# A small first load, a reordered root and one store fewer in the head of a fused scan and gated-MLP kernel

## The chip, the cores and the metric

The kernel runs on one core of one Trainium2 chip. The metric is the device time of one execution in microseconds; the median of three runs stands for a kernel. A core has TensorE (PE, matrix products), VectorE (DVE), ScalarE (ACT), GpSimd (POOL) and SyncE (SP). SyncE and ScalarE issue the kernel's plain loads, each from its own queue; the same 16 DMA engines move the data of both.

## The reference: what is computed

```python
xn = layernorm(x)                       # x: 2048 tokens x 448
s = 2.0 * real(hseq @ Cmat.T) + xn * Dskip   # hseq: h = Lam_bar * h + xn @ B_bar.T, token by token
h = sigmoid(xn @ w_gate) * (xn @ w_up)  # 448 -> 1792
g = silu(h @ w_down)                    # 1792 -> 448
out = x + s * g
```

Inputs and output are bfloat16. The change touches only how the first tokens are normalised and how the first columns of `w_gate` come in.

## The kernel before, in words

The 2048 tokens are 16 tiles of 128, in four chunks of 512. For each chunk TensorE does 14 gate and up steps (seven output pairs m for each of the two weights), the input product of the scan, the down product and the output product of the scan; VectorE does the scan itself and most evictions from PSUM.

**Order of work.** The kernel does not issue instructions directly. Each is added to a plan (`Plan.add`) with its engine, an estimated cost and the data that it reads and writes; `solve` then orders each engine's list by simulated times, and `emit` issues it. TensorE runs in program order. While `pl.seq` is set, which it is for the whole head, VectorE and ScalarE run in program order too. Loads go with `chain=True`, so each issuing queue keeps program order. `land` is the planner's figure for when a load arrives; it only steers the order.

**The head, chunk 0.** SyncE loads x tiles 0 and 2 (lines 402 and 404), ScalarE's queue tiles 1 and 3 (403 and 405). ScalarE's function table is loaded at 408. The first gate block is the first 256 of each half's 896 output columns. Its 448 input rows are seven groups of 64, and `load_w0` (line 374) brings them in four pieces: half 0 part A (three groups) and half 1 part A (four groups, on ScalarE's queue), then part B of half 0 (four groups) and of half 1 (three groups). Lines 409 to 412. Part A of both halves is what the matmuls marked "b" need; those marked "a" need part B too. After that SyncE issues the other gate blocks, more x tiles, and the up weights.

TensorE runs ten matmuls on constants at first (line 445). Tile 0's statistics are VectorE's (`stats`, 451 and 457) with the root on ScalarE (`root`, 485); tile 1's are ScalarE's (`act_mean` 489, `act_var` 493, `act_root` 497); tiles 2 and 3 are VectorE's with roots on ScalarE. A reciprocal (482) and a normalising step (531) on VectorE follow. Tile 0 is transposed by TensorE (569 and 571) into two banks, and ScalarE copies them out (579): first slots 4 to 6, after which the "b" matmuls run, then slots 0 to 3, after which the "a" matmuls run. Tiles 1 to 3 are transposed at 589 and 590, copied by ScalarE at 593, and shifted between partition halves by VectorE at 600. `last_tile` (826 and 827) does the gate matmuls of one tile: tile 0 "b", transposes of tile 1, tile 0 "a", transposes of tiles 2 and 3, then tiles 1, 2 and 3. From then on whole chunks are multiplied (808 and 809).

The small parameter rows, transposed by TensorE at 635 and 637 and copied at 642, are part of the head too. An output tile is finished in `yout` (1065 to 1067) and stored by SyncE (1056).

Of the kernel before, what the change touches and what calls it, by code (L numbers as in the profile page):

```python
# [14 lines left out]
ACT = mybir.ActivationFunctionType  # L15
# [3 lines left out]
D = 448  # L19
F = 1792  # L20
P = 128
H = 64
# [28 lines left out]
def dve2(n):  # L51
    return 0.067 + n / 1920.0


def dve1(n):
    return 0.067 + n / 960.0
# [17 lines left out]
class Plan:  # L74
# [10 lines left out]
    def add(self, eng, cost, fn, r=(), w=(), dma=0, lat=None, chain=False, name="", rate=230e3):  # L85
        o = Op()
        o.idx, o.eng, o.cost, o.fn, o.dma, o.name = len(self.ops), eng, cost, fn, dma, name
        o.lat = LAT.get(eng, 0.0) if lat is None else lat
        o.pre, o.suc, o.rate = {}, [], rate
        o.slot, o.land = None, 0.0  # L90
        if dma and eng != "POOL":
            o.slot, self.n_dma = self.n_dma, self.n_dma + 1
        o.start = o.end = None
        for k in r:
            if k in self.w:
                self._edge(self.w[k], o, True)
        for k in w:
            for q in self.r.get(k, ()):
                self._edge(q, o, False)
            if k in self.w:  # L100
                self._edge(self.w[k], o, True)
        for k in w:
            self.w[k] = o
            self.r[k] = []
        for k in r:
            if k not in w:
                self.r.setdefault(k, []).append(o)
        if chain or eng == "PE" or (eng in ("DVE", "ACT") and self.seq):
            key = ("chain", eng)
            if key in self.last_of:  # L110
                self._edge(self.last_of[key], o, None)
            self.last_of[key] = o
        self.ops.append(o)
        return o
# [132 lines left out]
def kernel(  # L247
# [18 lines left out]
    V, A, G, T, Q = nc.vector, nc.scalar, nc.gpsimd, nc.tensor, nc.sync  # L266
# [5 lines left out]
    def sbt(name, shape, dt=BF16):  # L272
        return sb.tile([P] + list(shape), dt, name=name)
# [10 lines left out]
    wgt = {"g": sbt("wG", [7, 896]), "u": sbt("wU", [7, 896])}  # L284
# [66 lines left out]
    add = pl.add  # L351
# [3 lines left out]
    def load(eng, key, nbytes, o, i, cost=0.45, r=(), rate=230e3, land=0.0):  # L355
        e = {"SP": Q, "ACT": A, "POOL": G}[eng]
        add(eng, cost, lambda: e.dma_start(out=o, in_=i), w=[key] if not isinstance(key, list) else key,  # L357
            r=r, dma=nbytes, chain=True, rate=rate).land = land

    def load_x(t0, n, q="SP", r=(), rate=230e3, land=0.0):  # L360
        load(q, [("x", t) for t in range(t0, t0 + n)], n * P * D * 2,
             x_all[:, t0:t0 + n, :], x_src[:, t0:t0 + n, :], r=r, rate=rate, land=land)
# [3 lines left out]
    def load_w(eng, k, half, b, r=(), rate=105e3, land=0.0):  # L366
        m0, m1 = BLK[k][b]
        ps = slice(half * H, half * H + H)
        c0 = half * 896
        load(eng, [("w", k, half, m) for m in range(m0, m1)], H * 7 * (m1 - m0) * P * 2,  # L370
             wgt[k][ps, :, m0 * P:m1 * P],
             wsrc[k][:, c0 + m0 * P:c0 + m1 * P].rearrange("(s p) f -> p s f", p=H), cost=0.65, r=r, rate=rate, land=land)

    def load_w0(eng, half, part, r=(), land=0.0):
        ps = slice(half * H, half * H + H)
        s0, c0 = (1 - half if part == "A" else half), half * 896
        n = 4 - s0
        load(eng, [("w", "g", half, m, part) for m in range(2)], H * n * 2 * P * 2, wgt["g"][ps, s0:7:2, 0:2 * P],
             wsrc["g"][:, c0:c0 + 2 * P].rearrange("(s p) f -> p s f", p=H)[:, s0:7:2, :], cost=0.5, r=r, rate=400e3, land=land)
# [21 lines left out]
    def load_p(eng, k, r=()):  # L401
        load(eng, ("vrow", k), D * 2, vrow[k:k + 1, :], (A_log_dt, A_Lambda_im, A_Lambda_re)[k].unsqueeze(0), cost=0.75 if eng == "POOL" else 0.45, r=r)
    load_x(0, 1, "SP")
    load_x(1, 1, "ACT")
    load_x(2, 1, "SP", rate=180e3)
    load_x(3, 1, "ACT", rate=180e3)
    load_p("SP", 2)
    add("ACT", 0.05, lambda: A.preload_act_table_set("sqrt_and_others"), w=["sqrttab"], lat=1.3, chain=True)
    load_w0("SP", 0, "A", land=5.7)
    load_w0("ACT", 1, "A", land=5.9)  # L410
    load_w0("SP", 0, "B", land=6.9)
    load_w0("SP", 1, "B", r=[("x", 1)], land=6.9)
    load_p("POOL", 0)
    load_p("POOL", 1)
    add("POOL", 0.15, lambda: G.memset(ident[:], 0.0), w=["ident"], chain=True)
    add("POOL", 0.4, lambda: G.affine_select(out=ident[:], in_=ident[:], compare_op=ALU.not_equal, fill=1.0, base=0,
                                             pattern=[[-1, P]], channel_multiplier=1), r=["ident"], w=["ident"], chain=True)
    add("POOL", 0.1, lambda: G.memset(wgt["g"][0:1, 0, 256:258], 0.0), w=[("w", "g", 0, m) for m in (2, 3)], chain=True)
    load_w("SP", "g", 0, 1, rate=400e3, land=8.8)
    load_w("SP", "g", 1, 1, rate=400e3, land=9.8)  # L420
    load_w("SP", "g", 0, 2, rate=400e3, land=11.2)
    load_w("SP", "g", 1, 2, rate=400e3, land=12.6)
    load_x(4, 2, land=14.0)
    add("POOL", 0.1, lambda: G.memset(halfc[:], 0.5), w=["consts"])
    add("POOL", 0.1, lambda: G.memset(negc[:], -1.0), r=["consts"], w=["consts"])
    add("POOL", 0.1, lambda: G.memset(expc[:], math.e), w=["expc"])
# [5 lines left out]
        w=[("xnw", t) for t in (1, 2, 3)])  # L432
# [16 lines left out]
    def bn(t):  # L449
        b = t % 3  # L450
        add("DVE", 0.56 if t < TPC else 0.6, lambda: V.bn_stats(out=bst[b][:], in_=x_all[:, t, :]),
            r=[("x", t)] + ([("xnT", 0, 3, "a")] if 3 < t < 8 else []), w=[("bst", b)])

    def aggr(t):
        b = t % 3
        o = (mvf if t < TPC else mv)[:, t, :]
        add("DVE", 0.1 if t < TPC else 0.16, lambda: V.bn_aggr(out=o, in_=bst[b][:]), r=[("bst", b)], w=[("mv", t)])

    def stats(t):
        bn(t)  # L460
        aggr(t)
# [22 lines left out]
    def root(t):  # L484
        add("ACT", 0.2, lambda: A.activation(sdb[:, t, :], mvf[:, t, 1:2], ACT.Sqrt, bias=epsc[:]),
            r=[("mv", t), "sqrttab", "epsc"], w=[("sd", t)], lat=0.16)

    def act_mean(t):
        add("ACT", 0.62, lambda: A.activation(junk[:], x_all[:, t, :], ACT.Identity, scale=-1.0 / D, accum_out=nmf[:, t, :]),
            r=[("x", t), "sqrttab"], w=[("nf", t), "junk"])  # L490
# [60 lines left out]
    def next_acc():  # L551
        a = acc_n[0] % 2
        acc_n[0] += 1
        return a
# [60 lines left out]
    def gate(keys, key):  # L615
        add("NONE", 0.0, lambda: None, w=list(keys) + (key if isinstance(key, list) else [key]), lat=0.0)
# [433 lines left out]
    def next_o():  # L1050
        o = o_n[0] % NO
        o_n[0] += 1
        return o

    def store(t, od, c0, c1, r0, r1, keys):
        add("SP", 0.45, lambda: Q.dma_start(out=out_flat[t * P + r0:t * P + r1, c0:c1], in_=od[r0:r1, :]),
            r=keys, w=[("store", t, c0, r0)], dma=(c1 - c0) * 2 * (r1 - r0))

    def yout(c, j, first=False):
        t = c * TPC + j  # L1060
        g, o, q = gt_of[c, j], next_o(), t % NXD
        a = next_acc()
        key, ok, od = ("acc", a), ("o", o, 0), o_t[o][:]
        y = y_mm(c, j, acc[a], key, 0, D, False, first)
        add("DVE", dve1(D), lambda: V.tensor_tensor(out=od, in0=y, in1=xd[q][:], op=ALU.add), r=[key, ("xd", q)], w=[ok])
        add("DVE", dve2(D), lambda: V.tensor_tensor(out=od, in0=od, in1=g_t[g][:], op=ALU.mult), r=[ok, ("gt", g)], w=[ok])
        add("DVE", dve2(D), lambda: V.tensor_tensor(out=od, in0=od, in1=x_all[:, t, :], op=ALU.add), r=[ok, ("x", t)], w=[ok])
        rows = (0, H, P) if c == 2 and j == 3 else (0, P)
        for r0, r1 in zip(rows, rows[1:]):
            store(t, od, 0, D, r0, r1, [ok])  # L1070

    def last_yout(c, j, banks):
        t = c * TPC + j
# [29 lines left out]
    u2 = slots0[2]  # L1103
    gate([("gu", u2)], [("gu", u2, 0), ("gu", u2, 1)])
    stats(0)
    act_mean(1)
    bn(2)
    root(0)
    act_var(1)
    recip(0, 1)  # L1110
    aggr(2)
    norm(0)
    act_root(1)
    root(2)
    stats(3)
    recip(1, 1)
    norm(1)
# [1 line left out]
    def split(t, keys, banks, eng, between=None):  # L1119
        pe_transpose(t, [(4, 7, keys[0], banks[0], eng[0]), (0, 4, keys[1], banks[1], eng[1])], between)  # L1120
# [5 lines left out]
    def between_copies():  # L1126
        copies.append(columns(acc[1][:, 400:412], ("acc", 1)))
        last_tile(0, "g", steps01, 0, "b")
        root(3)
    split(0, ak, ab, ("ACT", "ACT"), between_copies)  # L1130
    copies[0]()
    add("NONE", 0.0, lambda: None, r=["pv0", ("xn", 1)], w=["pv"], lat=0.0)
    first_slots(1, uk[0], ub[0], "ACT")
# [64 lines left out]
    for c in (2, 3):  # L1198
# [11 lines left out]
        whole(c)  # L1210

    yout(2, 0, True)
    yout(2, 1)
    free_banks = []
    for s in range(3):
# [50 lines left out]
```

## Time and profile before

| What | Value |
|---|---|
| median of three runs | 183.3 us (182.92 to 183.31) |
| span of the profiled execution | 181.5 us |
| TensorE busy | 177.1 us (98%) |
| VectorE busy | 166.4 us (92%) |
| ScalarE busy | 98.2 us (54%) |
| GpSimd busy | 37.6 us (21%) |
| TensorE clock granted | 1.000 over the whole span |
| bytes moved by DMA | 13.43 MB |

The profile gives the span, from the first to the last instruction; the time of an execution lies above it by what surrounds it (183.3 - 181.5 = 1.8 us against the median). Times inside the trace count from the start of the span. "Landing" of a load is the moment at which its completion semaphore is full. In the rows of the timeline the columns are start, duration, engine, line and operation, output and inputs, shapes and count, and in square brackets the idle time ahead and what ended it.

The loads of the head, from the trace:

| Load | Queue | Issued at | Landed at |
|---|---|---|---|
| x tile 0 | SP | 0.72 | 3.09 |
| x tile 1 | ACT | 0.73 | 3.25 |
| x tile 2 | SP | 1.19 | 3.88 |
| x tile 3 | ACT | 1.17 | 4.07 |
| gate half 1, part A | ACT | 1.69 | 5.92 |
| gate half 0, part A | SP | 2.02 | 6.05 |
| gate half 0, part B | SP | 2.81 | 6.28 |
| gate half 1, part B | SP | 3.47 | 7.20 |

### The profile page before, as it was taken

What the parts mean: (1) busy time and instruction counts of PE and PEld (TensorE: products, weight loads), DVE (VectorE), ACT (ScalarE), POOL (GpSimd) and SP (SyncE); (2) the same over time, 40 slices, a digit from 0 to 9 for tenths busy, and PEclk for the clock granted to TensorE, in tenths of its full rate; (3) what the DMA queues carried; (4) which work ended last, traced back from release to release, by engine and by line L of the source; (5) the groups of instructions that cost most, each with busy time, mean ns of one, the idle gap of its engine ahead of it and who ended that gap; (6) DMA issues with size and microseconds to landing.
All of it is one profiled execution on the core that took longest, in us unless ns stands there. A gap on an engine that the chain in (4) does not pass through costs nothing.

```text
span 181.5 us, 3611 instructions
## 1 busy us (share of the span) xinstructions
PE 177.1 (98%) x1404; PEld 88.2 (49%) x1411; DVE 166.4 (92%) x294; ACT 98.2 (54%) x162; POOL 37.6 (21%) x94
## 2 busy tenths in 40 slices
PE   8999999999999999999999999999999999999993
PEld 2664445664544444445554444444555444455552
DVE  3778799999989999999999999999999999999772
ACT  5799998857699985364155543348110533411100
POOL 6472468100018797000004100000000000000000
PEclk9999999999999999999999999999999999999999
DMA  5999999999000290000004900002000000002121
GB/s 133 227 224 229 160 165 207 252 242 257 23 0 0 52 148 6 0 4 0 0 2 88 143 0 0 4 0 69 7 4 0 25 27 28 1 0 76 47 65 47
DMA packets 30853, 13.43 MB, mean 74 GB/s; under 512 B 19442, under 2 KB 30835, under 8 KB 30835
## 3 DMA queue, kind: packets, MB, share of 16 engines
q1 hardware_dynamic: 30210, 12.83, 34.9%
q10 hardware_dynamic: 560, 0.36, 0.7%
q8 instruction: 11, 0.18, 0.5%
q14 instruction: 8, 0.06, 0.1%
q0 software_dynamic: 64, 0.00, 0.0%
HBM read 6.77 MB, written 1.84 MB: 47 GB/s over the span
## 4 chain that ended last, share of the span: by engine, by line
PE 94%; DMA 2%; SPq 1%; DVE 1%; issue 0%; DVEq 0%
PE gu L808 43%; PE gu L1024 15%; PE acc L1043 11%; PE acc L1024 9%; PE gu L896 8%; DMA wG<-in_B_w_gate_dram 2%; PE acc L899 2%; PE gu L882 2%; SPq L357 1%; PE gu L826 1%; PE acc L808 1%; PE gu L809 1%; DVE o_t L1085 0%; PE gu L827 0%; DVE o_t L1079 0%
## 5 line engine op out<-in xcount | busy, mean ns | idle before, releaser
L808 PE MATMUL gu<-xnT,wU 64*128 64x512 bf16 x196 | 45.8, 376 | 0.0
L809 PE MATMUL gu<-xnT,wU 64*128 64x512 bf16 x196 | 45.8, 376 | 0.0
L808 PE MATMUL gu<-xnT,wG 64*128 64x512 bf16 (+1 forms) x189 | 41.3, 360 | 0.0
L809 PE MATMUL gu<-xnT,wG 64*128 64x512 bf16 (+1 forms) x189 | 41.3, 360 | 0.0
L842 ACT ACTIVATE sig<-gu 128x1024 f32<-128x1024 f32 x21 | 21.3, 1019 | 24.4 <-PE gu L809 19.8
L1024 PEld LDWEIGHTS <-hF 128*128 128x128 bf16 x224 | 21.9, 98 | 20.6
L808 PEld LDWEIGHTS <-wU 64*128 64x128 bf16 x196 | 18.4, 94 | 22.9
L808 PEld LDWEIGHTS <-wG 64*128 64x128 bf16 x196 | 18.4, 94 | 19.9
L1024 PE MATMUL gu<-wd,hF 128*128 128x448 bf16 x140 | 28.0, 352 | 0.0
L845 DVE SCALAR_TENSOR_TENSOR hF<-sig,gu 128x1024 bf16<-128x1024 f32 x21 | 25.4, 1210 | 0.7 <-ACT sig L842 0.4
L1043 PE MATMUL acc<-cT,hT 128*128 128x448 bf16 (+2 forms) x119 | 22.9, 337 | 0.0
L963 DVE TENSOR_TENSOR_SCAN wv<-c_r,st,z 128x512 bf16<-128x512 f32 x18 | 22.8, 1273 | 0.0
L1030 ACT ACTIVATE g_t<-gu 128x448 bf16<-128x448 f32 x10 | 5.4, 540 | 27.7 <-PE gu L1024 16.8
L809 PEld LDWEIGHTS <-wU 64*128 64x128 bf16 x196 | 18.4, 94 | 0.0
L809 PEld LDWEIGHTS <-wG 64*128 64x128 bf16 x196 | 18.4, 94 | 0.0
L1024 PE MATMUL acc<-wd,hF 128*128 128x448 bf16 x84 | 16.9, 352 | 0.0
L1043 PEld LDWEIGHTS <-hT 128*128 128x128 bf16 x126 | 11.7, 98 | 9.9 <-issue 0.4
L896 PE MATMUL gu<-xnT,bT 128*128 128x512 bf16 x65 | 15.3, 379 | 0.4
L910 ACT CAST bus<-gu 128x1024 bf16<-128x1024 f32 x12 | 12.0, 1011 | 5.9 <-PE gu L882 5.3
L541 POOL COPY xn<-xn 128x448 bf16<-128x448 bf16 x12 | 7.5, 627 | 27.2 <-ACT xn L535 27.0
L916 ACT CAST bus<-acc 64x256 bf16<-64x256 f32 (+1 forms) x24 | 8.7, 368 | 4.8 <-PE acc L899 4.5
L535 ACT ACTIVATE xn<-x_all,nmr,rsd 128x448 bf16<-128x448 bf16 x12 | 8.8, 758 | 3.7 <-DVE xd L546 2.2
(162 smaller groups left out, 263.1 us busy)
## 6 DMA issues: line engine op xcount, KB each, us to landing
wd<-in_B_w_down_dram SPq DMA_DIRECT2D x2, 784.0 KB, 6.6
out_dram<-o_t SPq DMA_DIRECT2D x14, 112.0 KB, 1.7
wU<-in_B_w_up_dram SPq DMA_DIRECT2D x4, 224.0 KB, 8.4
x_all<-in_A_x_dram SPq DMA_DIRECT2D x2, 448.0 KB, 5.0
wG<-in_B_w_gate_dram SPq DMA_DIRECT2D x2, 336.0 KB, 5.4
wU<-in_B_w_up_dram SPq DMA_DIRECT2D x2, 336.0 KB, 8.5
wG<-in_B_w_gate_dram SPq DMA_DIRECT2D x2, 224.0 KB, 4.1
x_all<-in_A_x_dram SPq DMA_DIRECT2D x2, 224.0 KB, 7.7
```

What stands on the lines that cost most here:

```text
L535: add("ACT", 0.65, lambda: A.activation(o[:, 0:448], x_all[:, t, :], ACT.Identity, bias=nmr[:, t, :], scale=rsd[:, t, :]), r=[("x", t), (" ...
L541: add("POOL", 0.25 if n == H else 0.6, lambda: G.tensor_copy(out=o[:, D:D + n], in_=o[:, 0:n]), r=[("xn", b)], w=[("xnw", b)])
L808: T.matmul(bank[0][:, ts], lhsT=w_[0:H, s, ms], rhs=x[0:H, SL[s], ts], start=(s == 0), stop=(s == 6))
L809: T.matmul(bank[1][:, ts], lhsT=w_[H:P, (s + 1) % 7, ms], rhs=x[H:P, SL[s], ts], start=(s == 0), stop=(s == 6))
L842: add("ACT", act(1024), lambda: A.activation(th, gu[a][:], ACT.Tanh, scale=0.5), r=[("gu", a)], w=[tk])
L845: add("DVE", dve1(1024), lambda: V.scalar_tensor_tensor(out=ho, in0=th, scalar=1.0, in1=gu[a][:], op0=ALU.add, op1=ALU.mult), r=[("gu", a) ...
L896: T.matmul(gu[slots[pt]][:, i, :], lhsT=bT[:, kt, i, pt * P:pt * P + P], rhs=x[:, kt, :], start=(first and kt == 0), stop=(not first and k ...
L910: add("ACT", act(1024), lambda: A.copy(out=bus[u][:], in_=gu[slots[pt]][:]), r=key(pt), w=[("bus", u)])
L916: add("ACT", 0.36, lambda ns=ns, d=d, q=q, l=l, i=i: A.copy(out=bus[u][d, l, ns], in_=acc[a3[i]][q, 0:256]), r=[("acc", a3[i])] + ([("bus" ...
L963: dve(1.194, lambda k=k: V.tensor_tensor_scan(out=wv[:, k, :], data0=rb, data1=z[:, k, :], initial=(st[pt][:, k, :] if c else 0.0), op0=AL ...
L1024: T.matmul(d, lhsT=hF[c % 2][:, m, h, js], rhs=wd[:, ft, :], start=(ft == 0), stop=(ft == FT - 1))
L1043: T.matmul(y, lhsT=hT[c % 2][:, hm, js], rhs=cT[:, cm, c0:c1], start=(i == 0 and not skip_on_pe), stop=(i == 6))
```

## The change

Four things are done.

1. A load of 7 KB goes first on ScalarE's queue. It takes 32 columns (64 bytes) of 112 rows of `w_gate`: in each of the seven groups of 64 rows, every fourth row. Its target `scr` is read by nobody. x tile 1 is now second on that queue; x tile 3 comes after the table load.
2. Tile 0's root stands ahead of tile 1's mean; the roots of tiles 2 and 3 move back, to behind tile 0's first copy and behind its second copy.
3. Half 1 part B of the first gate block names x tile 0 where it named x tile 1, and a fill of two cells of `wG` on GpSimd goes. Several `land` figures change. The first gate block stays in the four pieces in which it was.
4. The output tile (2, 3) is stored in one piece where it was stored in two halves of 64 rows.

```diff
     load_x(0, 1, "SP")
-    load_x(1, 1, "ACT")
-    load_x(2, 1, "SP", rate=180e3)
-    load_x(3, 1, "ACT", rate=180e3)
+    scr = sbt("scr", [7, 32])
+    load("ACT", "scr", 16 * 7 * 64, scr[0:16, :, :],
+         B_w_gate.rearrange("(s e r) f -> r e s f", s=7, r=4)[0][:, :, 0:32], cost=0.5)
+    load_x(2, 1, "SP", land=3.7)
+    load_x(1, 1, "ACT", land=3.5)
     load_p("SP", 2)
     add("ACT", 0.05, lambda: A.preload_act_table_set("sqrt_and_others"), w=["sqrttab"], lat=1.3, chain=True)
+    load_x(3, 1, "ACT", land=4.3)
     load_w0("SP", 0, "A", land=5.7)
     load_w0("ACT", 1, "A", land=5.9)
-    load_w0("SP", 0, "B", land=6.9)
-    load_w0("SP", 1, "B", r=[("x", 1)], land=6.9)
+    load_w0("SP", 0, "B", land=6.4)
+    load_w0("SP", 1, "B", r=[("x", 0)], land=6.6)
...
-    add("POOL", 0.1, lambda: G.memset(wgt["g"][0:1, 0, 256:258], 0.0), w=[("w", "g", 0, m) for m in (2, 3)], chain=True)
-    load_w("SP", "g", 0, 1, rate=400e3, land=8.8)
+    load_w("SP", "g", 0, 1, rate=400e3, land=8.5)
...
-        rows = (0, H, P) if c == 2 and j == 3 else (0, P)
-        for r0, r1 in zip(rows, rows[1:]):
-            store(t, od, 0, D, r0, r1, [ok])
+        store(t, od, 0, D, 0, P, [ok])
...
     stats(0)
+    root(0)
     act_mean(1)
     bn(2)
-    root(0)
     act_var(1)
     recip(0, 1)
     aggr(2)
     norm(0)
     act_root(1)
-    root(2)
     stats(3)
...
         last_tile(0, "g", steps01, 0, "b")
-        root(3)
+        root(2)
     split(0, ak, ab, ("ACT", "ACT"), between_copies)
+    root(3)
     copies[0]()
```

The other `land` figures that change are those of the gate blocks after the first and of x tiles 4 and 5, each 0.2 or 0.3 lower.

More of the change, by code (lines that the diff above doesn't have):

```diff
@@ L417 @@
                                              pattern=[[-1, P]], channel_multiplier=1), r=["ident"], w=["ident"], chain=True)
-    add("POOL", 0.1, lambda: G.memset(wgt["g"][0:1, 0, 256:258], 0.0), w=[("w", "g", 0, m) for m in (2, 3)], chain=True)
-    load_w("SP", "g", 0, 1, rate=400e3, land=8.8)
[L420 to L423, printed above, removed]
+    load_w("SP", "g", 0, 1, rate=400e3, land=8.5)
+    load_w("SP", "g", 1, 1, rate=400e3, land=9.5)
+    load_w("SP", "g", 0, 2, rate=400e3, land=11.0)
+    load_w("SP", "g", 1, 2, rate=400e3, land=12.4)
+    load_x(4, 2, land=13.8)
     add("POOL", 0.1, lambda: G.memset(halfc[:], 0.5), w=["consts"])
```

## The prediction

> **What bounds the kernel now.** I read the shares of the page first, then the chain of work that ended last, then the chain's first 12 us, then the waits of that stretch.
>
> ```profile
> PE 177.1 (98%) x1404; PEld 88.2 (49%) x1411; DVE 166.4 (92%) x294; ACT 98.2 (54%) x162; POOL 37.6 (21%) x94
> ...
> PE 94%; DMA 2%; SPq 1%; DVE 1%; issue 0%; DVEq 0%
> ```
>
> TensorE is busy for 177.1 of 181.5 us and is 94% of the chain. The list of its matmuls has, after 7.25 us, only seven gaps of about 0.05 us. So a later stage gives nothing unless it has less TensorE work, and the change takes none away. What can move is the head. The chain there:
>
> ```profile
> 3.42 0.04 issue
> 3.47 3.74 DMA wG<-in_B_w_gate_dram
> 7.20 0.05 issue
> 7.25 0.23 PE gu L827
> ```
>
> The last piece of the first gate block (half 1, part B, line 412) is issued at 3.47 and lands at 7.20; at 7.25 the first matmul that needs it runs. In the waits:
>
> ```profile
> PEld L827 <- DMA wG<-in_B_w_gate_dram: 0.3, 1, 0.3
> ```
>
> TensorE had its pair partner at 6.88 (line 826), so the wait is 7.25 - 6.88 = 0.37 us. That is nearly all that an earlier landing can give before tile 0's own data are the limit. Behind the head, TensorE's lead survives: block 2 of the gate lands at 9.15 and is needed at 10.71, the first tanh starts at 11.85 (1.0 long) for a slot that TensorE takes up again at about 13.7, and VectorE sits 1.2 us idle at 171.61 before the last outputs. A gain or a loss in the head goes to the end one to one.
>
> **Part 1: the order of the statistics.** ScalarE's and VectorE's timeline of the head:
>
> ```profile
> 3.11 0.63 DVE L451 BATCH_NORM_STATS2 bst<-x_all 128x6 f32<-128x448 bf16 x1 [3.11 <-DMA x_all<-in_A_x_dram]
> 3.77 0.18 DVE L457 BATCH_NORM_AGGREGATE mvf<-bst 128x2 f32<-128x6 f32 x1
> ```
> ```profile
> 3.28 0.58 ACT L489 ACTIVATE junk<-x_all 128x448 bf16<-128x448 bf16 x1 [0.34 <-DMA x_all<-in_A_x_dram]
> 3.76 0.19 ACT L489 ACTIVATION_READ_ACCUMULATOR junk<-x_all 128x1 f32 x1
> 4.06 0.30 ACT L485 ACTIVATE sdb<-mvf,epsc 128x1 bf16<-128x1 f32 x1
> 4.26 0.65 ACT L493 ACTIVATE junk<-x_all,nmf 128x448 bf16<-128x448 bf16 x1
> ...
> 5.03 0.30 ACT L497 ACTIVATE sdb<-sqf,epsc 128x1 bf16<-128x1 f32 x1
> 5.23 0.28 ACT L485 ACTIVATE sdb<-mvf,epsc 128x1 bf16<-128x1 f32 x1
> 5.57 0.48 ACT L579 COPY xnT<-acc 128x384 bf16<-128x384 bf16 x1
> 5.95 0.30 ACT L485 ACTIVATE sdb<-mvf,epsc 128x1 bf16<-128x1 f32 x1
> 6.15 0.57 ACT L579 COPY xnT<-acc 128x512 bf16<-128x512 bf16 x1
> ```
>
> Tile 0's root (4.06) comes 0.11 after its aggregate ends (3.95). Tile 1's mean ends at 3.95 too, so it does not hold the root up: putting the root first saves nothing by itself. It puts tile 1's mean and variance behind it. Call T the landing of x tile 0, 3.09 in the semaphore records. Durations from the rows above: root at T+0.97, mean 0.20 later (as 4.06 to 4.26), variance 0.69 later (3.28 to 3.95 and 0.02), root of tile 1 0.77 later (4.26 to 5.03), copy of tile 0's b slots 0.20 later: T+2.83, that is 5.92 at T = 3.09 against 5.57 now. From there, with the spacings of now: the copy takes 0.48 and the b matmuls start 0.04 behind it, T+3.35; tile 1's transposes come 0.43 later (6.11 to 6.54), the waiting a matmuls 0.34 later (6.54 to 6.88): T+4.12 = 7.21. Moving root 2 behind the b copy takes 0.20 off ScalarE's queue before that copy, which is counted. Root 3 now stands behind the a copy: root 2 is 0.38 after the b copy, the a copy 0.20 after that, root 3 another 0.46 (the copy's spacing to its follower, 6.15 to 6.61): T+3.87, done at T+4.15; reciprocal and normalising of tile 3 end 0.69 later (0.09, 0.20, 0.40), T+4.84, against 7.28 now. Its transposes could start at T+4.89 = 7.98, which is just when they start now, and tile 1's matmuls follow 0.37 later, as 8.35 follows 7.98. So the new order spends all of ScalarE's slack: T+5.26 = 8.35, as now. **With the weights in time, the gain is 3.09 - T and nothing else.**
>
> **Part 2: who lands when.** x tile 0 loses its rival on ScalarE's queue: tile 1 moves one place back. In the packet records each of 16 DMA engines moves 8 rows of 896 bytes of each tile at 41 ns, so between T = 3.09 (nothing gained) and 3.09 - 8 x 0.041 = 2.76 (the rival gone). The tiny load puts seven pieces of 64 bytes per engine in its place; at the 25 ns of a 512-byte packet that is at most 0.18. I take the middle, 2.93; the end above 3.09 is in the rivals. The Trainium skill ("DMA: Bandwidth & Descriptors", Issuing engines are not separate DMA queues) says that loads of all issuing engines interleave on the same 16 DMA engines. By that rule the touch is itself in x tile 0's way, and the trace agrees that queues share: ScalarE's packets began at 1.93, among SyncE's, which began at 1.74.
>
> Tile 1 now lands between 3.25 (now) and 4.07 (the tile that has its place now) and is needed at T+1.17 = 4.10: hidden. Tile 2 keeps its place. Tile 3 is issued behind the table load, some 0.5 later: 4.57 for a statistics step that starts at 4.95: hidden. Gate half 1 part A moves from 1.69 to about 2.15, so it lands at worst at 6.37 instead of 5.92; it is needed at T+3.35 = 6.28 and could cost 0.1 there.
>
> **Part 3: does the touch bring the weights in earlier?** DMA share and bytes in two half microseconds of the head:
>
> ```profile
> 4.50:5.00 0.50, 0.50 (x2) 0.00 (x0) 0.50 (x5) 0.50 (x2) 0.00 (x0) 1.00 0.93 274
> 5.50:6.00 0.50, 0.50 (x10) 0.33 (x7) 0.43 (x4) 0.44 (x3) 0.00 (x0) 1.00 0.56 125
> ```
>
> (The last two columns are share and GB/s.) In the packet records 23 of 1,428 gate packets of 512 bytes between 3.3 and 7.2 took over 150 ns, up to 786, where the median is 27. Their excess is 8.0 us; over 16 engines 0.50 us. If all of it is first use of an address range and the touch pays it beforehand, the last piece lands at 6.70; if none, at 7.20. I take 6.95. Against it: 7 more long ones fall at 7.2 to 9.2 on the same rows, which had been read by then, and the first reads of the up weights (10.6 to 17) have none over 150 in their 512- and 768-byte packets. For it: they bunch where x and the gate are first read. The Trainium skill (same page, Latency and other measured facts) puts HBM's access latency at 0.2 us on average and 2 us under load. By it the long packets come of load, and a touch removes none of them.
>
> **The rest.** GpSimd's 0.09 us fill of two weight cells goes; SyncE passed that point at 4.1, long after it (3.15): nothing. One store of 112 KB replaces two of 56 KB for the tile before the last four; SyncE has slack there (last outputs bound by TensorE): nothing. The gate's block was in four pieces already. New landing figures steer only the planner; a changed order of ScalarE or VectorE later can only cost, since TensorE has no gaps left, bounded by what one late eviction shows (about 0.3).
>
> **Sum.** a matmuls at max(2.93 + 4.12, 6.95 + 0.05) = 7.05, 0.20 earlier; tile 1's at 2.93 + 5.26 = 8.19, 0.16 earlier. The span goes from 181.5 to 181.34. The median shown is 183.3, 1.8 above the profiled span for what lies around it; I hold that constant: 183.14, said as 183.15.
>
> **Rivals.**
> - **The weights stay the limit** (7.20, for the reasons against in part 3). Then TensorE still waits until 7.25 and nothing moves: 183.3. It also covers that the touch does not do what it is said to do.
> - **Full gain.** T = 2.76 and the last piece before 6.8: 0.33 to 0.37 off, 182.95. It needs both ends at once.
> - **The touch holds SyncE's queue.** The trace's issue at 3.47 waits on the semaphore that x tile 1 completes, the first of eight taken up again by the ninth load. With one load more, gate half 0 part B (issued at 2.81) becomes the ninth and would wait for the touch; all weights queue behind it on SyncE. The first pieces of x tile 0 land at 2.58, the whole of tile 1 on ScalarE's queue at 3.25. If the touch lands before 2.8 it costs nothing. At 3.25 the last piece comes 0.44 later, at 7.64, TensorE's wait ends at 7.69: 183.75. Two or three long packets in a row (0.3 to 0.4 each) on one engine would be enough. x tile 0 delayed by the same packets has the same sign.
>
> **Chances.** Forecast 0.42, weights as before 0.25, full gain 0.13, touch holds the queue or the planner's order costs 0.20. A measurement of this kernel tells about 0.2% (0.37 us) from no change. Beyond that lie half of the full gain and the tails of the others (single runs lie 0.39 apart): faster 0.22; most of the last case: slower 0.20; within: 0.58. Range: 182.8, the full gain with a little scatter, to 183.7, which takes in most of the last rival.
>
> **What would show it.** Right: x tile 0's statistics start before 3.0, tile 1's mean at T+1.17, tile 1's matmuls at T+5.26, no wait of TensorE on the gate load. Wrong: the wait on the gate load still ends at 7.2 or later (weights), or SyncE's issue of half 0 part B comes after 2.85 (queue), or TensorE has new gaps past 11 us (planner).

## The result and the profile after

The changed kernel takes 183.74 us (183.41 to 183.94, seven runs) against 183.22 (182.92 to 183.31) for the kernel before in the same runs: a ratio of 1.0025, 95% interval 1.0016 to 1.0034, slower by about 0.5 us. Line numbers of the kernel after are mostly two higher (826 and 827 are 828 and 829).

The span and the shares, first on the page of the kernel after:

```profile
span 182.2 us, 3610 instructions
...
PE 177.2 (97%) x1404; PEld 88.4 (49%) x1411; DVE 166.5 (91%) x294; ACT 97.9 (54%) x162; POOL 34.9 (19%) x93
...
PE 94%; DMA 3%; DVE 1%; issue 0%; DVEq 0%
```

TensorE's work is the same to 0.1 us, and DMA has 3% of the chain where it had 2%. The chain of the first 12 us, kernel after:

```profile
0.67 0.06 issue
0.73 2.29 DMA scr<-in_B_w_gate_dram
3.05 4.01 DMA wG<-in_B_w_gate_dram
7.10 0.23 PE gu L829
```

The chain runs through the small load itself: its landing at 3.02 lets a gate piece be issued at 3.05, which lands at 7.06. ScalarE's timeline, kernel after (the letters ACTq mark the issue of a load), shows which piece it is:

```profile
0.73 0.41 ACTq L357 DMA_DIRECT2D scr<-in_B_w_gate_dram  x1
1.17 0.45 ACTq L357 DMA_DIRECT2D x_all<-in_A_x_dram  x1
1.65 1.28 ACT L410 ACT_TABLE_LOAD   x1 [1.65 <-PEq L1250]
1.68 0.42 ACTq L357 DMA_DIRECT2D x_all<-in_A_x_dram  x1
3.05 0.69 ACTq L357 DMA_DIRECT2D wG<-in_B_w_gate_dram  x1
3.85 0.30 ACT L487 ACTIVATE sdb<-mvf,epsc 128x1 bf16<-128x1 f32 x1 [0.91 <-DVE mvf L459]
4.05 0.56 ACT L491 ACTIVATE junk<-x_all 128x448 bf16<-128x448 bf16 x1
...
5.72 0.46 ACT L581 COPY xnT<-acc 128x384 bf16<-128x384 bf16 x1
```

It is half 1 part A, the piece on ScalarE's own queue. It could have been issued at 2.10, behind x tile 3, and was issued at 1.69 in the kernel before. Its issue instruction waits for the completion semaphore that the small load uses: both issue records of the trace name semaphore 107. Eight such semaphores are given out in turn (107, 109, 110, 111, 113, 114, 115 and 117), and the ninth plain load takes up the first again. In the kernel before half 1 part A had the eighth (117) and half 1 part B was the ninth. With one load more, and x tile 3 behind the table load, half 1 part A is the ninth.

The turn is not the order of issue on the chip: half 0 part B, issued at 2.76, has a fresh one (115). Nor is it the order in which the kernel's text adds the loads: by that half 1 part A would be the eighth and half 0 part B the ninth. The kernel's own planner counts in that order (`if k - 8 in landed`, in `solve`), and so it too expected the wait on the other piece. What sets the turn, the runs don't tell; the records name it. TensorE pays, in the waits and the list of its matmuls, kernel after:

```profile
PE gu L829 <- DMA wG<-in_B_w_gate_dram: 0.7, 1, 0.7
```
```profile
7.10 0.23 PE L829 MATMUL gu<-xnT,wG 64*128 64x128 bf16 x1 [0.66 <-DMA wG<-in_B_w_gate_dram]
...
11.33 0.38 PE L810 MATMUL gu<-xnT,wG 64*128 64x512 bf16 x1
```

The same matmul in the kernel before:

```profile
10.71 0.38 PE L808 MATMUL gu<-xnT,wG 64*128 64x512 bf16 x1
```

Half 1 part A feeds the "b" matmuls. They begin at 6.23 with half 0 and stop until 7.10. The first whole-chunk matmul starts at 11.33 in the kernel after and 10.71 in the kernel before, 0.62 later. The last matmul ends at 179.05 against 178.43, again 0.62 later: all of the loss between these two executions is made in the head and carried to the end unchanged.

Two facts help to read what follows. First, **from the start of "b" to the first whole-chunk matmul TensorE takes 4.24 us when nothing holds it** (6.22 to 10.46 in e6 below, 6.51 to 10.74 in e5), so what exceeds that is a wait (e11 is an exception, told there): 0.36 in the kernel before (6.11 to 10.71), 0.86 after (6.23 to 11.33). Second, in the profiled executions compared, the time lies 1.78 above the span (183.94 over 182.16; 183.05 over 181.28). By that the profiled execution of the kernel before, with its span of 181.55, took 183.33: not the median of 183.2, but the slow end.

### The profile page after: what moved, and what is told of

It reads as the page before. It is cut to its first block, busy times and chain, and to the rows that moved or that the text cites. A ratio compares the mean times of both kernels' runs of the same rounds, so it can differ in the third digit from the quotient of the medians.

```text
span 182.2 us, 3610 instructions
## 1 busy us (share of the span) xinstructions
PE 177.2 (97%) x1404; PEld 88.4 (49%) x1411; DVE 166.5 (91%) x294; ACT 97.9 (54%) x162; POOL 34.9 (19%) x93
## 4 chain that ended last, share of the span: by engine, by line
PE 94%; DMA 3%; DVE 1%; issue 0%; DVEq 0%
PE gu L810 43%; PE gu L1026 15%; PE acc L1045 11%; PE acc L1026 9%; PE gu L898 8%; DMA wG<-in_B_w_gate_dram 2%; PE acc L901 2%; PE gu L884 2%; PE gu L828 2%; DMA scr<-in_B_w_gate_dram 1%; PE acc L810 1%; PE gu L811 1%; DVE o_t L1085 0%; PE gu L829 0%; DVE o_t L1079 0%
```

## The experiments

"Ratio" is to the kernel before, run on the same chip beside it, with its 95% interval; a ratio of 1.001 is 0.18 us.

| Kernel | Median us | Ratio | "b" starts | first whole-chunk matmul |
|---|---|---|---|---|
| before | 183.0 to 183.2 | 1 | 6.11 | 10.71 |
| after | 183.74 | 1.0025 [1.0016, 1.0034] | 6.23 | 11.33 |
| e1 no small load | 183.48 | 1.0019 [1.0011, 1.0028] | 6.61 | 10.84 |
| e2 tile 3 later | 183.78 | 1.0039 [1.0026, 1.0052] | 6.22 | 10.90 |
| e3 touch of up | 183.63 | 1.0032 [1.0017, 1.0047] | 6.25 | 10.98 |
| e4 ninth in before | 184.42 | 1.0098 [1.0062, 1.0133] | 6.49 | 11.14 |
| e5 roots alone | 183.34 | 1.0012 [1.0003, 1.0020] | 6.51 | 10.74 |
| e6 no wait | 183.40 | 1.0009 [0.9999, 1.0018] | 6.22 | 10.46 |
| e7 one row load fewer | 183.36 | 1.0016 [1.0000, 1.0032] | 6.22 | 10.81 |
| e8 the rest alone | 183.19 | 1.0002 [0.9993, 1.0010] | 6.33 | 10.56 |
| e9 before, weights sooner | 183.15 | 1.0005 [0.9997, 1.0013] | 6.36 | 10.59 |
| e10 e9, sooner still | 183.19 | 1.0007 [0.9999, 1.0016] | 6.08 | 10.31 |
| e11 e6 with touch of up | 183.12 | 1.0005 [0.9997, 1.0014] | 6.30 | 10.66 |
| e12 e6, old root order | 183.22 | 1.0009 [1.0001, 1.0018] | 6.40 | 10.64 |
| e13 after, old root order | 183.50 | 1.0030 [1.0013, 1.0048] | 6.47 | 10.89 |

The last two columns are of one profiled execution each; the ratio is of all runs.

**e1: the kernel after without the small load.** The first three lines of the diff's additions (`scr` and its load) are taken out again.

> The changed kernel without the small load, all else as changed. Theory A (the small load made gate half 1 part A the ninth load, and it waits on ScalarE's queue until the small load's semaphore, which it takes over, is full): with one load less it is the eighth again and takes a fresh semaphore; issued at about 1.7, landed at about 5.9, no wait of TensorE of 0.87 before the b matmuls. x tile 1 is first on ScalarE's queue again, so x tile 0 lands at 3.09 and the new order gains 3.09 - 3.09 = 0: 183.2, ratio to the kernel before 0.999 to 1.001. Theory B (the new order of the roots, or the planner's new order, costs the time): still 183.6 to 183.8. Theory C (the small load's packets disturb the other loads): 183.2 too; this run does not tell A from C.

Between the two figures. The wait is gone (half 1 part A issued at 1.66, landed at 5.57), but x tile 0 has its rival back and lands at 3.25, not 2.85. "b" then starts at 6.61, at T + 3.36, and waits for ScalarE's copy, not for weights. Two things changed at once, so e1 alone can't price the wait.

**e2: x tile 3 behind half 1 part A.** It moves back on ScalarE's queue, so that half 1 part A is the eighth load again; its statistics move behind tile 1's normalising step.

```diff
-    load_x(3, 1, "ACT", land=4.3)
     load_w0("SP", 0, "A", land=5.7)
     load_w0("ACT", 1, "A", land=5.9)
+    load_x(3, 1, "ACT", land=4.3)
...
     act_root(1)
-    stats(3)
     recip(1, 1)
     norm(1)
+    stats(3)
```

> The changed kernel with the small load kept, but gate half 1 part A issued ahead of x tile 3 on ScalarE's queue, so that x tile 3 is the ninth load, and tile 3's statistics put behind tile 1's normalising on VectorE, since that tile now lands late. Theory A: the gate piece is issued at about 1.7 and landed by 5.9; the b matmuls run at about 6.2 as their input allows; x tile 3 waits for x tile 0's semaphore (2.85) and lands at about 5.3; tile 3 is ready some 0.4 later than in the changed kernel, of which 0.3 to 0.4 is hidden: 182.9 to 183.2. Theories B and C: the order and the small load are both still there: 183.6 to 183.9.

A miss as a cure, and instructive. ScalarE's timeline, e2:

```profile
1.69 0.68 ACTq L357 DMA_DIRECT2D wG<-in_B_w_gate_dram  x1
2.88 0.35 ACTq L357 DMA_DIRECT2D x_all<-in_A_x_dram  x1
```

The wait moved to x tile 3, which takes up x tile 0's semaphore (109, full at 2.86); the small load's goes to half 1 part B. Half 1 part A landed at 5.89, and the "b" and "a" matmuls start at 6.22 and 6.99, as in e6. But half 1 part B landed only at 7.40, and "a" stops for it. TensorE's matmuls, e2:

```profile
6.99 0.23 PE L828 MATMUL gu<-xnT,wG 64*128 64x128 bf16 x1
7.44 0.23 PE L829 MATMUL gu<-xnT,wG 64*128 64x128 bf16 x1 [0.22 <-DMA wG<-in_B_w_gate_dram]
```

The transposes of tiles 2 and 3 follow at 7.99 where e6 has them at 7.55: 0.44 later, which is the whole difference of e2's 10.90 from e6's 10.46. The late x tile 3 alone would have cost about as much: issued at 2.88, it landed at 6.18, its normalising step ends at 8.17, and its transposes run at 8.23, where e6 has them at 7.78. So e2 doesn't tell the two apart.

**e3: the small load reads the up weights.** `B_w_gate.rearrange` becomes `B_w_up.rearrange`. **e11** is the same edit without the wait, on e6.

> The changed kernel with the small load taken from the up weights instead of the gate weights: same shape, same place, same semaphore. Theory A: only the semaphore counts: as the changed kernel, 183.6 to 183.9. If touching the gate's rows brings the gate pieces in earlier, they land 0.2 to 0.5 later here and the time is 183.9 to 184.3. If touching them disturbs, the time is below 183.5.

> The kernel of e6 (x tile 3 on SyncE's queue, so that the first gate piece on ScalarE's queue is issued without waiting), with the small load taken from the up weights instead of the gate weights. It tells apart, without the wait of the kernel after, whether reading rows of the gate weights ahead brings them sooner. If it does: the last gate piece lands 0.25 us or more later than the 6.57 of e6, and the time is 183.6 or more. If it doesn't: 183.3 to 183.5, as e6 with 183.40.

Reading rows of the gate ahead brings nothing. With the wait, e3 is where the kernel after is (1.0032 against 1.0025); without it, e11 is where e6 is (1.0005 against 1.0009). The last gate piece lands at 6.57 in e6 and 6.44 in e11. (In e11's profiled execution the "b" matmuls themselves take 0.13 longer, with no wait named: its 10.66 is not a matter of loads.) In the packet records of 3.3 to 7.2 us, the 512-byte gate packets over 150 ns are 15 to 23 of some 1,400 in the six kernels that touch the gate (after, e2, e6, e7, e12, e13) and 7 to 24 of some 1,500 in the nine that don't. So the counts show no effect of the touch. The Trainium skill ("DMA: Bandwidth & Descriptors", Latency and other measured facts) gives HBM's access latency as 0.2 us on average and 2 us at high load. The counts don't contradict that, but no run here shows that load is what makes these packets long.

**e4: the kernel before with a ninth load.** 64 bytes of `Dskip` are loaded on ScalarE's queue ahead of half 1 part A, nothing else.

```diff
+    scr = sbt("scr", [32])
+    load("ACT", "scr", 64, scr[0:1, :], A_Dskip.unsqueeze(0)[:, 0:32], cost=0.45)
     load_w0("ACT", 1, "A", land=5.9)
```

> The kernel before, with nothing of the change, plus one load of 64 bytes of Dskip that nobody reads, put between the table load and gate half 1 part A on ScalarE's queue. The gate piece becomes the ninth load and takes over the semaphore of x tile 1 (full at 3.25). Theory A: it is issued at about 3.3 instead of 1.69 and lands at about 7.2 instead of 5.92; the b matmuls start at about 7.25 instead of 6.11, and by the change's own example (7.10 cost 0.62) the loss is 0.6 to 0.9: 183.8 to 184.1. Theories B and C: none of the change is in it: 183.2, within 0.1.

The effect is there and larger than expected. ScalarE's timeline, e4:

```profile
1.69 0.51 ACTq L357 DMA_DIRECT2D scr<-in_A_Dskip_dram  x1
3.29 0.71 ACTq L357 DMA_DIRECT2D wG<-in_B_w_gate_dram  x1
4.04 0.58 ACT L491 ACTIVATE junk<-x_all 128x448 bf16<-128x448 bf16 x1 [1.10 <-DMA x_all<-in_A_x_dram]
```

The small load here touches no gate; apart from its own issue (0.51) it only uses up a turn. Half 1 part A is issued at 3.29 instead of 1.69, and a second cost shows: ScalarE's own first step, tile 1's mean, starts at 4.04 although x tile 1 landed at 3.27. That landing frees the blocked issue too, and the issue stands first in ScalarE's program: it runs from 3.29 to 4.00, and the mean behind it. In the kernel after that cost was hidden, because the issue ended at 3.74, ahead of the root at 3.85. In the profiled execution (184.09) the head accounts for 0.43 (11.14 against 10.71), the last matmul ends 0.47 later, and the span is 0.76 longer. The trace shows where the other 0.28 lies. At its end the program has SyncE wait for the shared semaphores one after the other, some 0.06 each. The last store here carries semaphore 107, the second of that list; in the kernel before it carries 117, the last. Five more waits follow its landing, and from the landing to the end of the span it takes 1.21 instead of 0.93. So the extra load costs twice, once by the turn in the head and once by the turn at the end. (The six kernels of the three pairs below all end on 117, as the kernel before does; e1 and e7 to e10, with one such transfer fewer, lose about 0.05 there.) Why the median is higher still is open: two of the six runs lie above 186.

**e5: the kernel before with the new root places alone** (the three root moves of the diff, nothing else).

> The kernel before with the new places of the three roots and nothing else: same loads, same semaphores. Theory A (the semaphore that gate half 1 part A takes over is the whole loss): 183.2, within 0.1. Theory B (the new order of the roots itself costs): by the spacings of the prediction the a matmuls of tile 0 come at T + 4.12 instead of T + 3.79 (6.88 at T = 3.09, where their input was ready), so 0.2 to 0.35 is lost wherever the weights are not later than that: 183.4 to 183.5, and no wait of TensorE on a load.

The order costs by itself: 1.0012, 0.22 us (interval 0.05 to 0.37). In the waits, e5:

```profile
PE gu L826 <- ACT xnT L579: 0.3, 1, 0.3
```

TensorE no longer waits for weights but for tile 0's copy. With T = 3.15 "b" starts at 6.51, T + 3.36 (the prediction had T + 3.35).

**e6: the wait taken from the kernel after.** x tile 3 goes to SyncE's queue, ahead of its gate pieces, so that half 1 part A is the eighth load; the ninth is half 0 part B, whose semaphore is free by then.

```diff
-    load_x(3, 1, "ACT", land=4.3)
...
     load_p("SP", 2)
+    load_x(3, 1, "SP", land=4.3)
```

> The changed kernel with the small load, the new order and all else kept, but x tile 3 issued on SyncE's queue ahead of the gate pieces, so that gate half 1 part A is the eighth load and half 0 part B, on SyncE's queue, the ninth. Gate half 1 part A is issued at about 1.7 and lands before 6.0; the pieces on SyncE's queue are issued 0.45 later than in the changed kernel (the last at 3.9, landing near 7.2). T = 2.85. Theory A alone: the loss is gone: 183.0 to 183.2. A and B together: x tile 0's 0.24 pays back most of the order's 0.33: 183.2 to 183.4. If the touch or the planner's later order were the cause: still 183.7.

ScalarE issues the piece at 1.69 (it lands at 5.36), and TensorE has no gap in the head. TensorE's matmuls, e6:

```profile
6.22 0.21 PE L828 MATMUL gu<-xnT,wG 64*128 64x128 bf16 x1
6.22 0.23 PE L829 MATMUL gu<-xnT,wG 64*128 64x128 bf16 x1
...
10.46 0.38 PE L810 MATMUL gu<-xnT,wG 64*128 64x512 bf16 x1
```

"b" starts when it did in the kernel after (6.23), but nothing stops it: 10.46 instead of 11.33. The same move of x tile 3 parts three pairs: after and e6 (1.0025 and 1.0009), e3 and e11 (1.0032 and 1.0005), e13 and e12 (1.0030 and 1.0009). That is 0.29, 0.49 and 0.38 us by the ratios. By the medians, each against the kernel before beside it, the three are 0.33, 0.34 and 0.28: e3 and e13 each have one run above 185, which the ratios contain. So the wait costs about 0.3 us. The two profiled executions of the first pair lie further apart (0.87) because after's is the slowest of its seven runs and e6's all but the fastest of its own.

**e7: one load fewer in another place.** Lambda's real row is not loaded (a fill on GpSimd gives constants instead, so that part of the computation is changed), and half 1 part B waits for that fill.

> The changed kernel without the load of Lambda_re (left out: the row is filled with a constant by GpSimd), and with the last gate piece behind a fill on GpSimd, so that gate half 1 part A is the eighth load and keeps its place on ScalarE's queue, and no piece of the gate is late. It shows the new order at its best: T = 2.85, chain of ScalarE alone. By T + 7.59 (the first whole-chunk gate matmul of the run without the touch, 10.84 at T = 3.25) that matmul comes at 10.44 and the time at 183.0 to 183.15. Theory A alone: 183.0 or less. If touch or planner cost: 183.5 and more.

Half 1 part A is issued at 2.14, without the wait. Half 1 part B lands at 7.30 and TensorE waits 0.3 for it. The interval (1.0000 to 1.0032) is too wide to tell it from e6 or from the kernel after.

**e8: the rest alone.** The store in one piece, the fill gone and the `land` figures, on the loads and roots of before.

> The changed kernel with the loads and the roots put back as they were: what is left is one store in place of two, the fill that goes, and the planner's landing figures. All theories of the head: 183.2, within 0.1. If the planner's new order or the store cost something: above 183.3.

Nothing: 1.0002. Its profile teaches more than its time. Loads and root places of the head are those of the kernel before, yet TensorE waits for no weights. TensorE's matmuls, e8 (lines one lower than before):

```profile
6.33 0.23 PE L825 MATMUL gu<-xnT,wG 64*128 64x128 bf16 x1
...
7.10 0.23 PE L825 MATMUL gu<-xnT,wG 64*128 64x128 bf16 x1
```

x tile 0 landed at 3.24 here and the last gate piece at 7.02, in time for "a" at 7.10. The 0.37 us wait stood in the profiled execution of before and not in this one; how often it comes, two executions can't tell.

**e9 and e10: the weights sooner, in the kernel before.** e9 moves Lambda's row to GpSimd's queue, e10 also moves half 1 part B to ScalarE's.

```diff
-    load_p("SP", 2)
...
-    load_w0("SP", 1, "B", r=[("x", 1)], land=6.9)
+    load_w0("ACT", 1, "B", land=6.6)
     load_p("POOL", 0)
     load_p("POOL", 1)
+    load_p("POOL", 2)
```

> The kernel before, with one edit: the load of Lambda's row (the third load on SyncE's queue) moves to GpSimd's queue, behind the columns' row and D's row. SyncE then issues its first gate piece about 0.38 us earlier, and no gate piece has to take over a semaphore that an earlier load still holds. If the landing of the last gate piece is what holds the first gate matmuls of the kernel before: up to 0.35 us less, 182.85 to 183.1. If those matmuls are held by the tiles' own order in the typical run: no change, 183.1 to 183.3. If the pieces land when the data's share of the DMA engines lets them, whenever they are issued, the last one lands at 6.9 to 7.3 all the same.

> The kernel of e9 with the second half's second piece issued on ScalarE's queue, right behind the first piece there, so that all of the first gate block is issued by about 3.1 us. Expected 182.85 to 183.2 if the last issue sets the last landing (it would land at 6.5 to 6.8 instead of 7.2); the same as e9 if it doesn't. Slower than e9 by up to 0.3 us if the second piece's issue on ScalarE's queue delays the mean of tile 0.

The last gate piece landed at 6.39 and 6.62 where it had been 7.20, and TensorE never waited for it; the time did not move (1.0005, 1.0007, both intervals hold 1). In e9 TensorE waits 0.3 for the moved row at 5.96 instead; TensorE's waits in e10 name no load at all. So an earlier landing, taken alone, is worth nothing that can be measured in the typical run.

**e12 and e13: the old root order,** on e6 (no wait) and on the kernel after (wait).

> The kernel of e6 (the small load first, x tile 3 on SyncE's queue, no gate piece waiting for a semaphore) with the roots in the order of the kernel before. x tile 1 lands at about 3.86 there, so tile 1's mean, which stands ahead of tile 0's root again, ends at about 4.55 and the root starts at 4.6, where e6 has it at T + 0.97 = 3.83. If the tiles' own order is the limit without the wait: the 'a' matmuls at 4.6 + 2.82 = 7.42 against 6.98, so 0.3 to 0.5 us slower than e6, 183.5 to 183.9. If the new order is what costs, and the old one is free of it: 0.1 to 0.3 us faster than e6, 182.9 to 183.2. If another thing limits the head (weights): as e6.

> The kernel after with the roots in the order of the kernel before, the first gate piece on ScalarE's queue still waiting for the small load's semaphore. If the wait (the piece lands at about 7.06) is the only limit of the head there, the order is hidden beneath it: as the kernel after, 183.6 to 183.9. If order and wait add up: different from the kernel after by as much as e12 differs from e6, 184.0 to 184.2 with the sign that the first theory of e12 has, 183.4 or less with the other.

e13 is as expected of the wait: 1.0030, no different from the kernel after. e12 refutes me. ScalarE's timeline, e12:

```profile
4.53 0.28 ACT L487 ACTIVATE sdb<-mvf,epsc 128x1 bf16<-128x1 f32 x1
...
5.87 0.48 ACT L581 COPY xnT<-acc 128x384 bf16<-128x384 bf16 x1
```

I had expected 0.3 to 0.5 over e6, and it is the same (1.0009 both). Its mean starts at 3.95 and its root at 4.53, as foreseen, but from the root to tile 0's copy it takes 1.34 (4.53 to 5.87) where the kernel before, from which I had the spacing, takes 1.51 (4.06 to 5.57, shown in the prediction). "a" runs at 7.17, not 7.42. Its head is 0.18 behind e6's (10.64 against 10.46), and the medians don't confirm even that. With x tile 1 late, the two orders cost the same within what these runs can tell.

## Why the prediction was wrong

The prediction said 183.15, a gain; the median came to 183.74, a loss, and above its range (to 183.7).

- **The step that failed** is in part 2: "Gate half 1 part A moves from 1.69 to about 2.15, so it lands at worst at 6.37", with a cost of at most 0.1. It was issued at 3.05 and landed at 7.06; TensorE stood idle 0.66 for it, and "b" to the first whole-chunk matmul took 0.86 more than its 4.24. The step counted its place in the queue and not its semaphore. In the medians the wait costs about 0.3 us.
- **The rival had the mechanism, but the wrong piece:** it counted the ninth load by the time of issue and found half 0 part B on SyncE. That its 183.75 is so close is luck: it let the touch land at 3.25 (it landed at 3.02), put the wait on the "a" matmuls, and counted from 7.25, a time that already held the 0.37. The trace of before could have told: each issue record names the semaphore that the load completes, and half 1 part A, sixth of the plain loads by time (Lambda's row among them), already had the eighth. The rival's saving clause ("if the touch lands before 2.8 it costs nothing") was then of no use, since the piece on ScalarE's queue was ready to go at 2.10. A chance of 0.20 was too low for one load more on semaphores that were all in use. The Trainium skill ("DMA: Bandwidth & Descriptors", Rules for kernel authors) says to dedicate a semaphore to a DMA. The runs show what sharing costs here, about 0.3 us in the medians.
- **The ScalarE chain was right to 0.04.** With T = 2.85 the root is at T + 1.00, tile 0's copy at T + 2.87 and, in e6 (T = 2.86), "a" at 6.99 = T + 4.13; the prediction had 0.97, 2.83 and 4.12. T came at 2.85 (2.93 forecast).
- **"The gain is 3.09 - T and nothing else" was wrong** in what it is measured against. It compared "a" with 7.25, a time that held the 0.37 wait of one execution. No run shows that wait to be worth anything in the median: e8's identical head has none, and e9 and e10 remove it for no gain. Against 6.88, "a" at T + 4.12 comes 0.1 later even at T = 2.85, and 0.33 later at the old T. e5 measures the latter as 0.22 us; e6, e11 and e12 together lie 0.14 above before, with intervals that reach 1 or nearly so.
- **The touch:** the 6.95 was between "all" and "nothing"; it is nothing (e3, e11). The 8.0 us of excess in part 3 is 7.1 when the 23 packets are summed above their median of 27 ns, 0.44 an engine; the forecast did not hang on it, since T + 4.12 was the later term. What its place in the queue does bring is x tile 0 at 2.85, because 7 KB instead of 112 KB goes beside it. e11 has that as well.
- **The rest** was rightly nothing (e8).

Shown: the wait and its price (three pairs, and e4 with a ninth load alone), that the touch brings no weights sooner, the new order's cost at late T (e5), the zero of the rest. Open: how the remaining 0.14 us of e6, e11 and e12 divides, what sets the turn of the semaphores, and e4's two longest runs. No kernel here was faster than the kernel before.

## What to carry to other kernels

Before adding a load, however small, read from the issue records of the trace which completion semaphore each load already uses, and don't count the loads in the order of time or of the text: the load that becomes one too many waits for another's landing, and with it everything behind it on its engine, arithmetic included. A wait seen in one profiled execution is a gain only if that execution's own time stands at the median; here its 0.37 us was not there in the profiled execution of another kernel with the same head. And where an engine's chain has been counted to be just in time, check what it is just in time for: the data's own limit, not a wait that may not be there.

## What was not expected of the hardware

A load whose issue is blocked on ScalarE's queue holds ScalarE's compute behind it: in e4 the issue ran from 3.29 to 4.00, and tile 1's mean started 0.77 after its data (4.04 against 3.27), where it starts 0.03 after in the kernel before (3.28 against 3.25). And the second load of the head matters to the first: x tile 0 landed at 2.85 to 2.88 in the eight kernels with 7 KB first on the other queue (after, e2, e3, e6, e7, e11, e12, e13), and at 3.08 to 3.25 in the seven with 112 KB there.
